# Attention and cosine router: router logits summed in the PSUM bank by token strips, and wide items' gates spread from bf16 parts

## The chip, the cores and the metric

The kernel runs on one core of a Trainium2 chip. The metric is device microseconds for one execution.

## The reference

An attention in which a query sees only the keys of its own cluster feeds a mixture of experts with a cosine router.

```
q_assign = argmax(q_n @ c_n.T); k_assign = argmax(k_n @ c_n.T)     # 16 clusters a head
scores = where(q_assign == k_assign, scale * q @ k.T, -1e9)         # 4 batches, 8 heads, 768 x 64
x = softmax(scores) @ v, put to (3072, 512)

logits = xn @ en.T / tau                    # xn, en: rows of length one; 8 experts
e = argmax(logits); gate = softmax(logits)[e]
out[token] = gate * (relu(x @ w1[e]) @ w2[e])                       # w1 512x1024, w2 1024x512
```

Everything is fp32.

## The kernel before, in words

The order of work on every engine is the order in which the program issues it (`tc.manual_schedule` over all five engines), so a wait on one engine holds up all that stands behind it there.

**Attention.** There are 16 pairs of heads, n = 4 b + nb for batch b. A pair has twelve units, done two at a time in six iterations (`it` 0 to 5). In an iteration PE makes the scores of the next two units (line 484), ScalarE takes their exponent (L495), PE attends two units (L506), and VectorE adds the exponents up (L525). Between them `between(n, it)` puts small pieces of other work: turning the keys and queries of later pairs, their cluster products (L396), and the router's work for the batch before, which is `route_pieces(b - 1)`. The sums over the keys are products with ones (L553), in `total`.

**The router's pieces.** When the four pairs of a batch are through, its rows lie turned in four tiles `xT[b, c]`, c = 0 to 3: 128 of the 512 features on the partitions, tokens along the row, in two halves of 384. `embT` holds the experts' vectors, 32 columns wide (8 used). `products(half)` makes four products of 384 columns, one per c, each into its own strip of 32 partitions of one bank (L628); ScalarE copies the bank to `pT` (L636). `logits(half)` turns this with three PE transposes into another bank (L641), and VectorE adds the four strips with one reduction into `lg` (L644). `choose` finds the best expert per token, marks it in `eq`, counts it in `cumx` on GpSimd, and subtracts the maximum from `lg`, which the gate needs later. For batches 0 to 2 these pieces stand at iterations (nb, it) = (0, 4), (0, 5), (1, 2), (1, 3) and (1, 4) of the batch that follows.

For the last batch there is no attention behind which to put them. `products(0)` stands at the end of the last iteration. Then the order is written out: the first early item's hidden layer, `total` of the last group, gate pieces of the first three batches (`gates[1]` to `gates[3]`, which go from VectorE to ScalarE and back), then

```
gates[3]()
weights1(E0[2])
logits(0)
read(0, NJ, P - SQ, P)
products(1)
hidden(E0[1], (0,))
logits(1)
choose()
```

**Banks.** `misc()` hands out two PSUM banks in turn to all small products: cluster products, totals, router products, transposes, tables, gates. Who writes a bank waits for the reader of its last use, two calls before.

**Experts.** After four early items, the list `later` holds 16 items: eight blocks of 128 tokens and eight sized (wide) items, of 272 tokens down to 160, as block, sized, sized, block, sized, ... For the sized ones the slots are laid out in pieces of 32 tokens with a quarter of the features, so that a piece's gate is needed on all four strips of 32 partitions. `pb.gates` brings the gates of all slots into `slot_gates` (128 x 22): 24 products (L988) give three bf16 parts of each gate, VectorE copies the bank to `g3` (L996) and adds the parts (L997, L998). `spread_gates` then makes `gates4` for the 14 columns of the sized items: 16 fp32 products with columns of the identity (L1187) and one VectorE copy (L1194). It is called once, inside `sized_result` of the first sized item (`later[1]`), after its last transposition from the bank (L1218) and ahead of the multiplication by `gates4` (L1234).

For each item the loop over `later` orders the second weights if it is sized (`order_w2`, L1159), turns the next item's rows, makes the hidden layer (L1174 sized, L1259 block), issues weight loads two items ahead on SP, and makes the result (L1209 sized, L1275 block).

Of the kernel before, what the change touches and what calls it, by code (L numbers as in the profile page):

```python
# [9 lines left out]
F32 = mybir.dt.float32  # L10
BF16 = mybir.dt.bfloat16
I32 = mybir.dt.int32
ALU = mybir.AluOpType
ACTF = mybir.ActivationFunctionType
AXX = mybir.AxisListType.X
# [3 lines left out]
P = 128  # L19

SQ = 32
# [13 lines left out]
def bc(ap, shape, axis):  # L35
    return ap.unsqueeze(axis).to_broadcast(shape)
# [3 lines left out]
def kernel(  # L40
# [12 lines left out]
    nc = tc.nc  # L53

    B, H, S, D = q.shape
    C = centroids.shape[1]
    E, DM = moe_expert_emb.shape
    F = moe_w1.shape[2]
    N = B * S
    NJ = S // P  # L60
    NHP = H // 2
    HS = S // 2
    NSLOT = N // P
    KD = DM // P
    KF = F // P
    NQ = P // SQ
# [11 lines left out]
    NS = -(-sum(WIDE) // NQ)  # L78
# [23 lines left out]
    ident = const.tile([P, P], F32, name="ident")  # L102
    identb = const.tile([P, P], BF16, name="identb")
    cnB = const.tile([P, NHP, 2 * C], F32, name="cnB")
    embT = const.tile([P, KD, 2 * C], F32, name="embT")
# [38 lines left out]
    smp = ctx.enter_context(tc.tile_pool(name="smp", bufs=2))  # L144
# [32 lines left out]
    def misc():  # L177
        return bank("misc", psM)
# [282 lines left out]
    xT = {}  # L461
# [156 lines left out]
    def route_pieces(b):  # L618

        own = slice(NJ * b, NJ * b + NJ)  # L620
        t = {"sq": sq_all[:, own], "lg": lg_all[:, own]}
        U = NJ // 2

        def products(half):

            bk = misc()
            for c in range(KD):
                nc.tensor.matmul(  # L628
                    bk[2 * C * c : 2 * C * c + 2 * C, 0:HS],
                    lhsT=embT[:, c],  # L630
                    rhs=xT[b, c][:, half],
                    start=True,
                    stop=True,
                )
            t["pT", half] = smp.tile([P, HS], F32, tag="pT", name="pT")
            nc.scalar.copy(t["pT", half], bk[:, 0:HS])  # L636

        def logits(half):
            bk = misc()
            for u in range(U):  # L640
                nc.tensor.transpose(  # L641
                    bk[:, P * u : P * u + P], t["pT", half][:, P * u : P * u + P], ident
                )
            nc.vector.tensor_reduce(  # L644
                t["lg"][:, U * half : U * half + U],
                bk[:, 0:HS].rearrange("p (u c e) -> p u e c", c=KD, e=2 * C)[:, :, 0:E],
                axis=AXX,
                op=ALU.add,
            )

        def read(j0, j1, c0=0, c1=P):
            if "xr" not in t:
                t["xr"] = xp.tile([P, NJ, NQ, P], F32, tag="xr", name="xr", bufs=1)
            rows = x_rows[S * b + P * j0 : S * b + P * j1].rearrange("(j p) x -> p j x", p=P)
            if c1 - c0 == P:
                nc.sync.dma_start(
                    out=t["xr"][:, j0:j1].rearrange("p j w x -> p j (w x)"), in_=rows
                )
                return
            for w in range(NQ):  # L660
                nc.sync.dma_start(
                    out=t["xr"][:, j0:j1, w, c0:c1], in_=rows[:, :, P * w + c0 : P * w + c1]
                )

        def norms(j):
            junk = smp.tile([P, DM], F32, tag="junk", name="junk", bufs=1)
            nc.scalar.activation(
                junk,
                t["xr"][:, j].rearrange("p w x -> p (w x)"),
                ACTF.Square,  # L670
                accum_out=t["sq"][:, j : j + 1],
            )

        shp = [P, NJ, E]

        def choose():
            s0 = NJ * b
            mx = smp.tile([P, NJ], F32, tag="mx", name="mx")
            sel = smp.tile(shp, BF16, tag="sele", name="sele")
            pm = smp.tile([P, NJ], BF16, tag="pme", name="pme")  # L680
            nc.vector.tensor_reduce(mx, t["lg"], axis=AXX, op=ALU.max)
            nc.vector.tensor_tensor(sel, t["lg"], bc(mx, shp, 2), ALU.is_equal)
            nc.vector.tensor_tensor(sel, sel, bc(prefe, shp, 1), ALU.mult)
            nc.vector.tensor_reduce(pm, sel, axis=AXX, op=ALU.max)
            nc.vector.tensor_tensor(eq[:, s0 : s0 + NJ], sel, bc(pm, shp, 2), ALU.is_equal)
            for s in range(s0, s0 + NJ):
                nc.gpsimd.tensor_tensor(cumx[:, s + 1], cumx[:, s], eq[:, s], ALU.add)
            nc.vector.tensor_tensor(t["lg"], t["lg"], bc(mx, shp, 2), ALU.subtract)

        return products, logits, read, norms, choose  # L690

# [60 lines left out]
    class Places:  # L752
# [230 lines left out]
        def gates(self, to):  # L983

            m = to.shape[1]
            bk = misc()[:, 0 : 3 * m]
            for s in range(self.slots):
                nc.tensor.matmul(  # L988
                    bk,
                    lhsT=self.oh[:, s],  # L990
                    rhs=self.rg[:, s].rearrange("p t k -> p (t k)"),
                    start=(s == 0),
                    stop=(s == self.slots - 1),
                )
            g3 = self.tile([P, 3, m], F32, f"g3{m}")
            nc.vector.tensor_copy(g3.rearrange("p t k -> p (t k)"), bk)  # L996
            nc.vector.tensor_tensor(to, g3[:, 0], g3[:, 1], ALU.add)  # L997
            nc.vector.tensor_tensor(to, to, g3[:, 2], ALU.add)  # L998
# [182 lines left out]
            nc.scalar.activation(d["hT"][:, f, 0:C], bk, ACTF.Relu)  # L1181

    def spread_gates():
        bk = misc()[:, 0 : NQ * NS]
        for w in range(NQ):
            for to in range(0, P, SQ):
                nc.tensor.matmul(  # L1187
                    bk[to : to + SQ, NS * w : NS * w + NS],
                    lhsT=ident[:, SQ * w : SQ * w + SQ],
                    rhs=slot_gates[:, 0:NS],  # L1190
                    start=True,
                    stop=True,
                )
        nc.vector.tensor_copy(  # L1194
            gates4.rearrange("p k w -> p w k"), bk.rearrange("p (w k) -> p w k", w=NQ)
        )

    def sized_result(it):

        d, C, n = mo[it], CAPS[it.j], WIDE[it.j]  # L1200
        ys = d["ys"] = szp.tile([P, max(WIDE), P], F32, tag="ys", name="ys")
        cut = KF - 2
        bks = {}

        def products(g, fs):
            if g not in bks:
                bks[g] = misc() if g >= 2 else bank("y_ps", psY)
            for f in fs:
                nc.tensor.matmul(  # L1209
                    bks[g][:, 0:C],  # L1210
                    lhsT=d["w2"][:, f, P * g : P * g + P],
                    rhs=d["hT"][:, f, 0:C],
                    start=(f == 0),
                    stop=(f == KF - 1),
                )

        def turn_back(g):
            nc.vector.transpose(  # L1218
                ys[:, 0:n, SQ * g : SQ * g + SQ],
                bks[g][:, 0 : SQ * n].rearrange("p (u t) -> p u t", t=SQ),  # L1220
            )

        products(0, range(cut))
        products(1, range(cut))
        for g in range(2):
            products(g, range(cut, KF))
            turn_back(g)
        for g in range(2, KD):
            products(g, range(KF))
            turn_back(g)  # L1230
        u0 = FIRST[it.j]
        if it is later[1]:
            spread_gates()
        nc.vector.tensor_tensor(  # L1234
            ys[:, 0:n], ys[:, 0:n], bc(flat(gates4)[:, u0 : u0 + n], [P, n, P], 2), ALU.mult
        )
# [85 lines left out]
    later = items[KA:]  # L1322
# [7 lines left out]
    def between(n, it):  # L1330
        b, nb = divmod(n, NHP)
# [22 lines left out]
        if b > 0:  # L1354
            if nb == 0 and it == 3:
                route[b - 1] = route_pieces(b - 1)
            products, logits, read, norms, choose = route.get(b - 1, (None,) * 5)


            m = NJ * nb + it  # L1360
            if m in (8, 11, 14):
                read((m - 8) // 3 * 2, (m - 8) // 3 * 2 + 2)
            if m in (15, 16, 18, 19, 21, 22):
                norms((15, 16, 18, 19, 21, 22).index(m))
            if (nb, it) == (0, 4):
                products(0)
            elif (nb, it) == (0, 5):
                products(1)
            elif (nb, it) == (1, 2):
                logits(0)  # L1370
            elif (nb, it) == (1, 3):
                logits(1)
            elif (nb, it) == (1, 4):
                choose()
        if n == NP - 1 and it == 4:
# [12 lines left out]
        if (n, it) in first:  # L1388
            w, j, i = first[n, it]
# [14 lines left out]
    with tc.manual_schedule(engines=by_hand):  # L1404
# [153 lines left out]
        for i, it in enumerate(later):  # L1558
# [30 lines left out]
                result(it)  # L1589
            if i == 0:  # L1590
                fetch(later[2])
            if i + 2 < LAST and it.kind != "sized":
                weights2(later[i + 2])
        if later[-1].kind == "sized":
# [44 lines left out]
```

## Time and profile before

| | |
|---|---|
| median of 8 runs | 721.09 us (720.54 to 724.16) |
| the profiled execution | 723.32 us, of which the span of its instructions is 721.5 us |
| granted TensorE clock over the span | 0.989 |
| busy: PE, VectorE, ScalarE, GpSimd | 97%, 53%, 37%, 37% |
| attention | up to about 341 us; the last PE product ends near 714 us |

How to read it: PE is TensorE's matmul, PEld its weight load, DVE VectorE, ACT ScalarE, POOL GpSimd, SP the engine that issues most transfers. A row of a group has the line, the engine, the operation, the tile written and those read, the shape and count, then the busy time, the mean length of one, and the engine's idle time ahead of them with what ended it. In the chain of what ended last each row has its start, the length of its slot, the engine and line, and the number of records; "issue" there is time in which the engine waited for nothing that the profile shows. In a row of busy time by stretch the last three figures are PE's granted clock, the busy share of the DMA engines and GB/s. An fp32 product shows as two weight loads and two matmul records, a bf16 product as one of each; a transposition shows as one of each.

### The profile page before, as it was taken

The page shows a single profiled execution, that of the slowest core. Times are in us where ns is not written, and L with a number is a line of the kernel's source. Part 1 is how long each engine was busy: PE and PEld are TensorE (multiplying, and loading weights), DVE is VectorE, ACT ScalarE, POOL GpSimd, SP SyncE. Part 2 cuts the span into 40 slices and gives each one's busy share as a digit, 9 for nine tenths or more (in the row PEclk, how much of TensorE's full clock was granted, in tenths as well). Part 3 has the DMA queues.
Part 4 walks back from the last instruction along what each step waited for, and adds up shares of the span by engine and source line. Part 5 has one row for each costly group of instructions (what it writes and reads, how often), then busy time and mean ns, then how long its engine had stood idle before and what let it go on. Part 6 is the DMA issues. An engine that isn't in the chain of part 4 may idle for free.

```text
span 721.5 us, 16021 instructions
## 1 busy us (share of the span) xinstructions
PE 701.7 (97%) x6462; PEld 458.3 (64%) x6462; DVE 381.7 (53%) x665; ACT 267.9 (37%) x454; POOL 263.7 (37%) x402
## 2 busy tenths in 40 slices
PE   7999999999999999999999999899999999999995
PEld 3444444444444444454966677797979797979693
DVE  4588887998979998998583111221030303031210
ACT  4556555577556655666315110101011111111111
POOL 2122221322224231444134446536355454535312
PEclk9899999999999999999999999999999999999998
DMA  9446556766547678669799977166848586869350
GB/s 145 72 68 108 104 100 96 143 146 112 96 88 154 128 144 164 141 179 332 176 306 351 332 261 273 36 252 237 298 168 302 213 315 218 313 234 332 131 217 28
DMA packets 244123, 135.53 MB, mean 188 GB/s; under 512 B 207808, under 2 KB 207810, under 8 KB 244044
## 3 DMA queue, kind: packets, MB, share of 16 engines
q1 hardware_dynamic: 237852, 121.28, 62.4%
q0 software_dynamic: 6016, 13.12, 5.2%
q8 instruction: 53, 0.87, 0.5%
q14 instruction: 26, 0.21, 0.1%
q10 hardware_dynamic: 176, 0.05, 0.0%
HBM read 115.92 MB, written 13.12 MB: 179 GB/s over the span
## 4 chain that ended last, share of the span: by engine, by line
PE 82%; issue 6%; DVE 5%; DMA 4%; POOL 1%; another core or an unknown queue 1%; ACT 1%; POOLq 0%; SPq 0%; DVEq 0%; ACTq 0%
PE s_ps L484 19%; PE o_ps L506 16%; PE h_ps L1259 10%; PE y_ps L1275 9%; PE h_ps L1174 9%; PE misc L1209 5%; PE y_ps L1209 5%; PE x_ps L1174 3%; DMA out_dram<-ys,spidx 3%; DVE acc L525 2%; PE misc L553 2%; PE misc L396 2%; PE misc L628 1%; DMA k<-in_k_dram 1%
## 5 line engine op out<-in xcount | busy, mean ns | idle before, releaser
L495 ACT ACTIVATE prob<-s_ps 128x768 f32<-128x768 f32 x192 | 153.4, 811 | 96.7 <-PE s_ps L484 76.8
L484 PE MATMUL s_ps<-qT,kT 64*64 64x384 f32 x1536 | 158.2, 486 | 0.0
L506 PE MATMUL o_ps<-prob,v 64*64 64x385 f32 x1536 | 144.5, 491 | 0.0
L525 DVE TENSOR_TENSOR acc<-acc,prob 128x768 f32<-128x768 f32 x128 | 125.2, 978 | 8.5 <-DVE acc L525 0.5
L506 PEld LDWEIGHTS o_ps<-prob,v 64*64 64x64 f32 x1536 | 54.9, 134 | 71.3 <-issue 60.0
L1259 PE MATMUL h_ps<-xTm,w1s 128*128 128x128 f32 x768 | 88.5, 275 | 1.7 <-issue 1.7
L1259 PEld LDWEIGHTS h_ps<-xTm,w1s 128*128 128x128 f32 x768 | 87.6, 192 | 4.1 <-issue 3.3
L539 POOL TENSOR_TENSOR o_sum<-o_sb 128x385 f32<-128x385 f32 x30 | 32.1, 1071 | 153.7 <-ACT o_sb L530 153.7
L1218 DVE STREAM_TRANSPOSE ys<-y_ps 128x256 f32<-128x256 f32 (+4 forms) x16 | 6.7, 416 | 154.0 <-PE y_ps L1209 153.0
L1275 PE MATMUL y_ps<-w2s,hT 128*128 128x512 f32 x192 | 85.0, 594 | 1.0 <-ACT hT L1266 1.0
L1050 POOL DMA_INDIRECT out_dram<-ys,spidx x56 | 56.9, 1016 | 76.6 <-DVE ys L1234 61.9
L484 PEld LDWEIGHTS s_ps<-qT,kT 64*64 64x64 f32 x1536 | 57.7, 134 | 38.1 <-issue 34.9
L1174 PE MATMUL h_ps<-xTs,w1s 128*128 128x272 f32 (+7 forms) x384 | 74.5, 351 | 1.0 <-ACTq L1539 1.0
L1266 ACT ACTIVATE hT<-h_ps 128x512 f32<-128x512 f32 x24 | 14.3, 596 | 160.8 <-PE h_ps L1259 118.4
L1174 PEld LDWEIGHTS h_ps<-xTs,w1s 128*128 128x128 f32 x384 | 67.7, 193 | 8.7 <-issue 2.9
L484 PE MATMUL s_ps<-hot 64*64 64x384 bf16 x768 | 66.1, 327 | 2.3 <-ACT prob L495 1.3
L574 POOL COPY inv<-inv 32x12 f32<-32x12 f32 x120 | 43.0, 358 | 55.0 <-DVE inv L571 50.6
L1039 POOL DMA_INDIRECT xs<-x_rows,gpidx x56 | 56.1, 1003 | 17.1 <-issue 16.8
L1275 PEld LDWEIGHTS y_ps<-w2s,hT 128*128 128x128 f32 x192 | 35.4, 190 | 41.8 <-issue 39.2
L484 PEld LDWEIGHTS <-hot 64*64 64x64 bf16 x768 | 24.1, 107 | 40.0 <-issue 38.9
L1209 PE MATMUL misc<-hTs,w2o 128*128 128x272 f32 (+7 forms) x256 | 48.0, 346 | 0.0
L1209 PE MATMUL y_ps<-hTs,w2o 128*128 128x272 f32 (+7 forms) x256 | 48.0, 346 | 0.0
(264 smaller groups left out, 690.2 us busy)
## 6 DMA issues: line engine op xcount, KB each, us to landing
w1s<-in_moe_w_dram SPq DMA_DIRECT2D x18, 2048.0 KB
w2s<-in_moe_w_dram SPq DMA_DIRECT2D x18, 2048.0 KB
v<-in_v_dram SPq DMA_DIRECT2D x128, 48.0 KB
q<-in_q_dram SPq DMA_DIRECT2D x60, 96.0 KB
k<-in_k_dram SPq DMA_DIRECT2D x60, 96.0 KB
x_rows<-xb SPq DMA_DIRECT2D x60, 96.0 KB
xr<-x_rows SPq DMA_DIRECT2D x9, 512.0 KB
w1s<-in_moe_w_dram SPq DMA_DIRECT2D x4, 1024.0 KB
```

Source lines behind the costliest of these rows:

```text
L484: nc.tensor.matmul(s_ps[D * half : D * half + D, h, 0:HS], lhsT=l[rows, half], rhs=r[rows], start=part == (1 if len(parts) < 2 else 0), st ...
L495: nc.scalar.activation(d["prob"][:, :, 0:HS], d["s_ps"][:, :, 0:HS], ACTF.Exp, scale=scale)
L506: nc.tensor.matmul(g["o_ps"][D * h : D * h + D, half, 0:HE], lhsT=ld[n]["v"][keys, j, h], rhs=d["prob"][keys, h, 0:HE], start=(j == 0), st ...
L525: nc.vector.tensor_tensor(g["acc"], g["acc"], d["prob"][:, :, 0:HS], ALU.add)
L539: add(t["o_sum"][:, hq], t["o_sb"][:, 0], t["o_sb"][:, 1], ALU.add)
L574: nc.gpsimd.tensor_copy(inv2[M * to : M * to + M, :, i % 2], inv[M * i : M * i + M])
L1039: nc.gpsimd.indirect_dma_start(out=to, out_offset=None, in_=of, in_offset=bass.IndirectOffsetOnAxis(ap=at, axis=0), bounds_check=n - 1, oo ...
L1050: inst = nc.gpsimd.indirect_dma_start(out=to, out_offset=bass.IndirectOffsetOnAxis(ap=at, axis=0), in_=of, in_offset=None, bounds_check=n - 1,
L1174: nc.tensor.matmul(bk, lhsT=w1s[it.slot][:, c, P * f : P * f + P], rhs=d["xT"][:, c, 0:C], start=(c == 0), stop=(c == KD - 1),)
L1209: nc.tensor.matmul(bks[g][:, 0:C], lhsT=d["w2"][:, f, P * g : P * g + P], rhs=d["hT"][:, f, 0:C], start=(f == 0), stop=(f == KF - 1),)
L1259: nc.tensor.matmul(bk[:, m : m + P], lhsT=w1s[it.slot][:, c, f0 + m : f0 + m + P], rhs=d["xT"][:, P * c : P * c + P], start=(c == 0), stop ...
L1275: nc.tensor.matmul(bk, lhsT=d["hT"][:, P * c : P * c + P], rhs=w2s[it.slot][:, c], start=(c == 0), stop=(c == KF - 1),)
```

## The change

**Router.** `products(*halves)` now takes one or two halves. A strip of 32 partitions no longer holds one c, but the tokens of one quarter of each 128 (32 w to 32 w + 31); the four c are added up in the bank. So there are 16 products, of 192 columns for both halves together or of 96 for one. `logits(*halves)` is a single VectorE transposition of 32x32 blocks from that bank to a new tile `lt`; the copy on ScalarE, the PE transposes and the reduction are gone, and `choose` reads `lt`. For batches 0 to 2 both halves go together, products at (0, 4) and logits at (0, 5). For the last batch the calls stay as they were, one half at a time.

**Gates of the wide items.** `gates` copies the bank also as bf16 to `g3b`; `spread_gates` spreads the three bf16 parts (42 columns) with the bf16 identity instead of the fp32 gates (14 columns), and VectorE copies the bank and adds the parts. It is called after the first later item's result instead of inside the first sized item's.

```
-        def products(half):
-
-            bk = misc()
+        def products(*halves):
+
+            J = U * len(halves)
+            bk = t["bk", halves[0]] = misc()
             for c in range(KD):
-                nc.tensor.matmul(
-                    bk[2 * C * c : 2 * C * c + 2 * C, 0:HS],
-                    lhsT=embT[:, c],
-                    rhs=xT[b, c][:, half],
-                    start=True,
-                    stop=True,
-                )
-            t["pT", half] = smp.tile([P, HS], F32, tag="pT", name="pT")
-            nc.scalar.copy(t["pT", half], bk[:, 0:HS])
-
-        def logits(half):
-            bk = misc()
-            for u in range(U):
-                nc.tensor.transpose(
-                    bk[:, P * u : P * u + P], t["pT", half][:, P * u : P * u + P], ident
-                )
-            nc.vector.tensor_reduce(
-                t["lg"][:, U * half : U * half + U],
-                bk[:, 0:HS].rearrange("p (u c e) -> p u e c", c=KD, e=2 * C)[:, :, 0:E],
-                axis=AXX,
-                op=ALU.add,
+                x = xT[b, c][:, halves[0] : halves[0] + len(halves)]
+                x = x.rearrange("p k (u w t) -> p w k u t", w=NQ, t=SQ)
+                for w in range(NQ):
+                    nc.tensor.matmul(
+                        bk[SQ * w : SQ * w + SQ, 0 : SQ * J],
+                        lhsT=embT[:, c],
+                        rhs=x[:, w],
+                        start=(c == 0),
+                        stop=(c == KD - 1),
+                    )
+
+        def logits(*halves):
+            J = U * len(halves)
+            if "lt" not in t:
+                t["lt"] = smp.tile([P, NJ, SQ], F32, tag="lt", name="lt", bufs=1)
+            nc.vector.transpose(
+                t["lt"][:, U * halves[0] : U * halves[0] + J].rearrange("p j e -> p (j e)"),
+                t.pop(("bk", halves[0]))[:, 0 : SQ * J],
             )
...
+            lt = t["lt"][:, :, 0:E]
+            nc.vector.tensor_reduce(mx, lt, axis=AXX, op=ALU.max)
+            nc.vector.tensor_tensor(sel, lt, bc(mx, shp, 2), ALU.is_equal)
...
+            nc.vector.tensor_tensor(t["lg"], lt, bc(mx, shp, 2), ALU.subtract)
...
             g3 = self.tile([P, 3, m], F32, f"g3{m}")
+            if self.part == 1 and m == self.blocks:
+                self.g3b = self.tile([P, 3, m], BF16, "g3")
+                nc.vector.tensor_copy(self.g3b.rearrange("p t k -> p (t k)"), bk)
...
     def spread_gates():
-        bk = misc()[:, 0 : NQ * NS]
+
+        bk = misc()[:, 0 : NQ * 3 * NS].rearrange("p (w t k) -> p w t k", w=NQ, t=3)
         for w in range(NQ):
             for to in range(0, P, SQ):
                 nc.tensor.matmul(
-                    bk[to : to + SQ, NS * w : NS * w + NS],
-                    lhsT=ident[:, SQ * w : SQ * w + SQ],
-                    rhs=slot_gates[:, 0:NS],
+                    bk[to : to + SQ, w],
+                    lhsT=identb[:, SQ * w : SQ * w + SQ],
+                    rhs=pb.g3b[:, :, 0:NS],
                     start=True,
                     stop=True,
                 )
-        nc.vector.tensor_copy(
-            gates4.rearrange("p k w -> p w k"), bk.rearrange("p (w k) -> p w k", w=NQ)
-        )
+        parts = mop.tile([P, 3, NS, NQ], F32, tag="parts4", name="parts4", bufs=1)
+        nc.vector.tensor_copy(parts.rearrange("p t k w -> p w t k"), bk)
+        nc.vector.tensor_tensor(gates4, parts[:, 0], parts[:, 1], ALU.add)
+        nc.vector.tensor_tensor(gates4, gates4, parts[:, 2], ALU.add)
...
-        if it is later[1]:
-            spread_gates()
...
             if (nb, it) == (0, 4):
-                products(0)
+                products(0, 1)
             elif (nb, it) == (0, 5):
-                products(1)
-            elif (nb, it) == (1, 2):
-                logits(0)
-            elif (nb, it) == (1, 3):
-                logits(1)
+                logits(0, 1)
...
             if i == 0:
                 fetch(later[2])
+                spread_gates()
```

More of the change, by code (lines that the diff above doesn't have):

```diff
@@ L680, in choose @@
             pm = smp.tile([P, NJ], BF16, tag="pme", name="pme")
-            nc.vector.tensor_reduce(mx, t["lg"], axis=AXX, op=ALU.max)
-            nc.vector.tensor_tensor(sel, t["lg"], bc(mx, shp, 2), ALU.is_equal)
+            lt = t["lt"][:, :, 0:E]
+            nc.vector.tensor_reduce(mx, lt, axis=AXX, op=ALU.max)
+            nc.vector.tensor_tensor(sel, lt, bc(mx, shp, 2), ALU.is_equal)
             nc.vector.tensor_tensor(sel, sel, bc(prefe, shp, 1), ALU.mult)
@@ L687, in choose @@
                 nc.gpsimd.tensor_tensor(cumx[:, s + 1], cumx[:, s], eq[:, s], ALU.add)
-            nc.vector.tensor_tensor(t["lg"], t["lg"], bc(mx, shp, 2), ALU.subtract)
+            nc.vector.tensor_tensor(t["lg"], lt, bc(mx, shp, 2), ALU.subtract)
         return products, logits, read, norms, choose
```

## The prediction

> **What bounds the kernel now.** I read the page's busy times first, to see which engine could set the end:
>
> ```profile
> PE 701.7 (97%) x6462; PEld 458.3 (64%) x6462; DVE 381.7 (53%) x665; ACT 267.9 (37%) x454; POOL 263.7 (37%) x402
> ```
>
> PE is busy from end to end, so what leaves PE's queue is worth its full length, unless PE then waits for somebody. A share is not yet a place, so next come the groups kept apart by form, for the lines the change touches:
>
> ```profile
> L628 PE MATMUL misc<-xT,embT 128*32 128x384 f32 x64 | 6.8, 498 | 0.0
> L641 PE MATMUL misc<-ident,pT 128*128 128x128 f32 x24 | 4.3, 286 | 0.0
> L644 DVE TENSOR_REDUCE lg_all<-misc 128x24 f32<-128x96 f32 x8 | 1.9, 238 | 3.8 <-PE misc L641 3.8
> L1187 PE MATMUL misc<-slot_gates,ident 128*32 128x14 f32 x32 | 1.1, 186 | 3.0 <-issue 3.0
> ```
>
> An fp32 matmul is two records (32 products give 64). Means overlap, so what a group costs PE's queue is read from the chain that ended last, in order of time. Around batch 2's router work:
>
> ```profile
> 276.16 0.78 PE misc L628 x8
> 276.94 1.45 PE o_ps L506 x16
> ...
> 286.10 0.81 PE misc L553 x16
> ...
> 291.56 0.48 PE misc L641 x3
> 292.03 1.45 PE o_ps L506 x16
> ...
> 298.65 1.29 PE o_ps L506 x16
> ```
>
> The reader should see the slot of each insertion, and that the attend after it takes 1.45 instead of 1.29: an insertion costs 0.16 more. Then the gate spread, by the same view:
>
> ```profile
> 449.74 0.32 PE misc L1187 x25
> 450.06 0.56 issue
> 450.62 0.17 PE misc L1187
> 450.79 0.54 issue
> 451.33 0.22 PE misc L1187 x3
> 451.56 1.89 issue
> 453.44 0.29 PE misc L1187 x3
> 453.73 6.96 PE h_ps L1174 x24
> ```
>
> Sixteen tiny products hold PE from 449.74 to 453.73, 3.99 us. The busy time by stretch says what follows:
>
> ```profile
> 449.00:454.00 5.00, 2.01 (x37) 1.38 (x36) 0.52 (x2) 0.00 (x0) 2.01 (x3) 0.95 0.24 67
> 454.00:458.00 4.00, 4.00 (x13) 3.24 (x13) 3.97 (x10) 0.38 (x1) 1.92 (x2) 0.64 0.05 16
> ```
>
> The clock column falls to 0.64 after the stop, and the next 24 hidden products take 6.96 where the 24 from 462.42 take 5.18: 1.78 more. Last, VectorE's timeline at the end of attention, needed for a wait that the change makes:
>
> ```profile
> 352.63 0.21 DVE L717 STREAM_TRANSPOSE gate_t<-gate_p 128x32 f32<-128x32 f32 x1
> 352.77 0.21 DVE L644 TENSOR_REDUCE lg_all<-misc 128x24 f32<-128x96 f32 x1
> ```
>
> **Batches 0 to 2 of the router.** Before, per batch: two product slots of 0.78 + 0.16 and two turns of 0.48 + 0.16, together 3.16 us of PE. After: 16 products of 192 columns in one slot. The nearest row is L553, also 192 columns on 32-column strips: 16 records in 0.81, where its records in the trace start four at a time, 0.162 apart. The change has 32 records, four groups more: 0.81 + 4 x 0.162 = 1.46, plus 0.16 = 1.62. Bounds: 1.46 if the insertion costs nothing extra; and, if sums within a bank kept strips from overlapping, 32 x 0.162 = 5.2. I take 1.62, since L553's strips overlap as wanted and L396 reads runs of 32 elements no slower than whole rows. Saved: 1.54 per batch, 4.62 in three.
>
> ScalarE loses two copies of 0.48 per batch. VectorE loses two reductions of 0.24 and gains a transpose of 128x192: 0.38 by the L1218 form of that size, also from a bank. All that lies beside PE; if that cover went, VectorE would still come out 0.1 ahead. `choose` reads the same 48 numbers with a longer stride; bounds -0.1 and +0.3 for its three reads, taken as 0. What is late next is VectorE's additions: in its timeline it idles only 0.2 and 0.47 between 204 and 251, and the chain runs over it from 224.8 to 264.8. Of the 1.28 that PE loses in that pair of heads, VectorE can follow with 0.67 + 0.48 = 1.15. With a little more for ScalarE's waits I take **4.4** of the 4.62.
>
> **The last batch.** Here the halves stay apart: `products(0)`, later `logits(0)`, `products(1)`, a hidden half, `logits(1)`. A half is now 32 records of 96 columns. [...] The L1187 row above has 25 records in 0.32, 13 ns each, on four strips. The trace decides: four records per 0.081 (half of L553's 0.162), 0.65 plus L553's start of 0.16, 0.81 against 0.78 now. [...]
>
> The new cost is a wait. `misc` has two banks in turn. Before: `products(0)` X, `total` Y, `logits(0)` X, `products(1)` Y. After, `logits(0)` takes no bank, so `products(1)` gets X, which is free only when VectorE has transposed the first half, and that stands behind `gates[3]` in its queue: L717 ends at 352.84, the transpose of 128x96 takes 0.28 (0.35 at 160 columns, 0.38 at 192, carried down), with a hand-over 353.2. PE arrives at 350.98 and waits 2.2 us; queued behind it are the hidden half of the second early item and everything after. `products(1)` then ends at 354.06 instead of 352.09: +1.97. The second turn (0.33 in the chain at 355.86) goes: net **+1.65**. `choose` comes earlier, but nobody on PE waits for it. SP's and POOL's queues keep their order and only shift with PE.
>
> Could the pause halve the clock? A stop of 1.74 at 407.67 did not (clock 1.00 in that stretch), the one at 450 did; 2.2 lies between. [...]
>
> **The gate spread.** After: 16 bf16 products of 42 columns, behind the result of the first later item. The nearest row is L1024, 16 of 44 columns: 0.21 in the chain, with the hidden block after it 0.20 longer, so 0.41. Bounds: -0.2 and the 3.99 of today. If the stop belongs to this burst of 64 fp32 loads and products, 3.99 + 1.78 - 0.41 = **5.36** is gained; L1024's 32 instructions show no stop. VectorE gains a copy of 0.23 (as L996) ahead of a gate that ScalarE needs only at 420.49, then a copy of 0.49 (as L1032) and two additions of about 0.2, and it loses the 0.22 copy L1194. The eight weight-ordering copies (L1159, 2.8 us at 415.37) now stand behind them and behind the result: about 421.6 to 424.4. Their reader is PE at 435.07, so 10 us of hidden products cover it; without cover it would be 4 to 6 us.
>
> **Sum.** -4.4 + 1.65 - 5.36 = -8.1 us. It is made against the profiled execution (723.32, span 721.5); the median of 8 runs is 2.2 lower, so a stop such as the 1.74 at 407.67 may be missing there, but not all of the 7.5 that the two stops and the slow clock cost. I take the sum off the median: 721.09 - 8.1 = 713.0, say 713.2.
>
> **Rivals.** *The stop is not the burst's.* The records say only "issue", and the stop at 407.67 has no burst; both come while transfers fill the DMA engines (share 0.95 in 403 to 410, 1.02 in 446 to 449). Then it returns elsewhere or was in the profile alone: -4.4 + 1.65 = -2.75, so 718.4. *VectorE bounds attention.* It is 90% busy there; if batches 0 to 2 give only 1.0, the sum is -4.7: 716.4. Against: the chain runs over PE before 204 and after 264.8. *Slower: the new product bursts stop PE.* Each is 64 loads and products in one go, as L1187's was. At 3.6 + 1.8 us each, and with the old stop staying, one gives 718.4 + 5.4 = 723.8, three 734.6; it decides from one stop without the gain at the spread, or two with it. Against: wide products drain slowly, and L553's 32 instructions run without a gap. *The change does not do what it says*: the spread's fp32 products vanish in any case, so only the sizes are in doubt.
>
> **How the numbers follow.** All as worked out 0.50 (713.2, own range 711.3 to 715); stop stays or is not in ordinary runs 0.30 (717 to 720); VectorE bound 0.08; bursts that stop PE 0.12 (above 722). Range 711.3 to 720.0 leaves out the last case and a little at the low end. A measurement of this kernel can tell about 0.2%, 1.4 us, from no change. Faster 0.82, same 0.07, slower 0.11.
>
> **What would show it.** Right: one L628 slot per batch near 1.46 and none of L641; attends of 1.29 there; a PE gap of about 2 us before the second half's products, released by VectorE; the spread under 0.5 us at about 420, and clock 1.0 near 450. Wrong: pauses marked "issue" in or after the L628 bursts, VectorE in the chain through all of attention, or a stop still near 450.

## The result, and the profile after

The changed kernel takes 715.3 us (median of 11 runs, 712.97 to 720.36) where the kernel before takes 721.6 (median of 32): a ratio of 0.9914, 95% interval 0.9897 to 0.9931, or 6.2 us less (5.0 to 7.4). The forecast was 713.2, so the direction and the range held, the sum promised 2 us more than came, and the time lies just above 715, where the case "all as worked out" ended. The profiled execution took 718.94 us with a span of 717.2, against 723.32 and 721.5.

The busy times come first, as before:

```profile
PE 694.8 (97%) x6518; PEld 456.8 (64%) x6518; DVE 382.0 (53%) x665; ACT 264.3 (37%) x446; POOL 262.8 (37%) x402
```

PE has lost 6.9 us of work and still fills 97% of the span, so PE still sets the end. The changed lines, in the groups kept apart by form (after the bar: busy time, mean ns of one; then the idle time before them):

```profile
L632 PE MATMUL misc<-xT,embT 128*32 128x192 f32 x96 | 4.5, 329 | 0.0
L632 PE MATMUL misc<-xT,embT 128*32 128x96 f32 x64 | 1.7, 249 | 2.1 <-DVE lt L644 2.1
L644 DVE STREAM_TRANSPOSE lt<-misc 128x192 f32<-128x192 f32 x3 | 1.0, 339 | 0.0
L644 DVE STREAM_TRANSPOSE lt<-misc 128x96 f32<-128x96 f32 x2 | 0.5, 262 | 1.0 <-PE misc L632 1.0
L1198 DVE COPY parts<-misc 128x168 f32<-128x168 f32 x1 | 0.5, 468 | 6.4 <-PE misc L1190 6.4
```

The products of batches 0 to 2 waited for nobody; those of the last batch waited 2.1 us for VectorE's transpose. The chain that ended last shows the slot of batch 0 (start, length, what), and the places where the two turns used to stand:

```profile
109.95 1.44 PE misc L632 x32
111.39 1.45 PE o_ps L506 x16
112.85 1.61 PE s_ps L484 x24
114.46 1.29 PE o_ps L506 x16
...
125.06 1.29 PE o_ps L506 x16
...
127.97 1.29 PE o_ps L506 x16
```

One slot of 1.44, one attend of 1.45 behind it, and the attends where turns were inserted are back at 1.29. Now the last batch, by the chain, by PE's waits (total, times, longest) and by the busy time of stretches (PE, PEld, DVE, ACT, POOL, then the granted clock, DMA share, GB/s):

```profile
345.26 0.21 DVE gate_t L716
345.47 0.18 DVE lt L644
...
345.69 0.87 PE misc L632 x32
346.56 5.39 PE h_ps L1261 x32
```
```profile
PE misc L632 <- DVE lt L644: 2.1, 1, 2.1
```
```profile
344.00:346.50 2.50, 0.81 (x33) 0.66 (x33) 1.15 (x6) 0.81 (x2) 0.00 (x0) 1.00 0.54 80
346.50:350.00 3.50, 3.50 (x21) 3.50 (x18) 1.40 (x7) 0.00 (x0) 1.19 (x6) 0.54 0.30 52
```

The chain leaves PE here and runs over VectorE: the gate's last step (L716), the transpose (L644), and only then the products. Right behind the pause the clock column falls to 0.54, and the hidden half of 32 products takes 5.39. This fall is what the prediction left out. Last, the spread and the place at 450:

```profile
409.06 6.95 PE y_ps L1277 x16
416.01 0.21 PE misc L1190 x16
416.22 5.70 PE h_ps L1176 x24
...
438.41 7.33 PE misc L1213 x32
445.75 5.18 PE h_ps L1176 x24
```
```profile
450.00:454.00 4.00, 4.00 (x20) 3.51 (x19) 4.00 (x9) 1.06 (x4) 2.06 (x2) 1.00 0.05 16
```

The spread takes 0.21, the hidden block behind it 5.70, and where PE had stood for 3.99 us the first sized item's products now run straight into the next hidden block, at full clock.

The two traces can be cut at PE instructions that both have: the first cluster product (L396) of each pair of heads, and the first y product of each sized item (L1209, now L1213). The stretches between the cuts, in us:

| stretch | before | after | difference |
|---|---|---|---|
| up to the second pair of heads | 25.04 | 22.32 | -2.7 |
| batches 0 to 2 | 279.36 | 274.44 | -4.9 |
| last batch, the early items, up to the first sized result | 130.51 | 134.16 | +3.65 |
| from that result to the next | 34.26 | 28.48 | -5.8 |
| the next four sized results | 152.90 | 158.08 | +5.2 |
| the rest | 99.47 | 99.68 | +0.2 |

The second, third and fourth differences are the change. The first is not: in the profile of before the clock was halved from 16.6 to 23.4 us, in that of after it was not, and of the seven variants below three have no such stretch and four have one (what decides it is told with the clock below). Nor is most of the fifth, which holds a stop of 2.04 us that lasts 0.65 in two of the variants and that the others do not have:

```profile
601.19 0.60 ACT L1268 ACTIVATE hT<-h_ps 128x512 f32<-128x512 f32 x1 [7.77 <-remote]
601.84 2.86 PE L1277 MATMUL y_ps<-w2s,hT 128*128 128x512 f32 x4 [2.04 <-ACT hT L1268]
```

PE waits here for ScalarE, which itself starts 4.8 us after the end (596.36) of the hidden product that it reads. The clock is halved until 606.2, and the stretch from one sized item's first y product to the next takes 39.68 where it takes 35.67 in before, 35.66 or 35.67 in five variants, and 36.6 in the two with the short stop. No run ties this stop to the change. The difference of the two profiled executions, 4.4 us, is therefore a sum of chances as well as of the change; the stages and the medians have to be read apart.

### The profile page after: what moved, and what is told of

Its sections match the earlier page's. It is cut to its first block, busy times and chain, and to the rows that moved or that the text cites. A ratio compares the mean times of both kernels' runs of the same rounds, so it can differ in the third digit from the quotient of the medians.

```text
span 717.2 us, 16122 instructions
## 1 busy us (share of the span) xinstructions
PE 694.8 (97%) x6518; PEld 456.8 (64%) x6518; DVE 382.0 (53%) x665; ACT 264.3 (37%) x446; POOL 262.8 (37%) x402
## 4 chain that ended last, share of the span: by engine, by line
PE 80%; DVE 5%; issue 5%; DMA 4%; another core or an unknown queue 2%; ACT 1%; POOL 1%; SPq 1%; POOLq 0%; DVEq 0%; ACTq 0%
PE s_ps L484 19%; PE o_ps L506 15%; PE y_ps L1277 9%; PE h_ps L1176 9%; PE h_ps L1261 9%; PE misc L1213 5%; PE y_ps L1213 5%; DMA out_dram<-ys,spidx 3%; PE x_ps L1176 3%; PE misc L553 2%; PE misc L396 2%; DVE acc L525 2%; PE misc L632 1%; DMA k<-in_k_dram 1%
## 5 line engine op out<-in xcount | busy, mean ns | idle before, releaser
L484 PE MATMUL s_ps<-qT,kT 64*64 64x384 f32 x1536 | 156.0, 482 | 0.0
L506 PE MATMUL o_ps<-prob,v 64*64 64x385 f32 x1536 | 142.0, 486 | 0.0
L1261 PE MATMUL h_ps<-xTm,w1s 128*128 128x128 f32 x768 | 90.4, 279 | 1.3 <-issue 1.3
L1261 PEld LDWEIGHTS h_ps<-xTm,w1s 128*128 128x128 f32 x768 | 89.1, 195 | 3.0 <-issue 2.6
L1277 PE MATMUL y_ps<-w2s,hT 128*128 128x512 f32 x192 | 87.3, 605 | 3.8 <-ACT hT L1268 3.1
L484 PEld LDWEIGHTS s_ps<-qT,kT 64*64 64x64 f32 x1536 | 56.0, 133 | 38.0 <-issue 34.9
L1176 PE MATMUL h_ps<-xTs,w1s 128*128 128x272 f32 (+7 forms) x384 | 72.9, 346 | 1.1 <-ACTq L1537 1.1
L1213 PE MATMUL misc<-hTs,w2o 128*128 128x272 f32 (+7 forms) x256 | 48.2, 346 | 0.1
L1213 PE MATMUL y_ps<-hTs,w2o 128*128 128x272 f32 (+7 forms) x256 | 48.0, 346 | 0.0
```

The costliest lines, as they stand in the source:

```text
L484: nc.tensor.matmul(s_ps[D * half : D * half + D, h, 0:HS], lhsT=l[rows, half], rhs=r[rows], start=part == (1 if len(parts) < 2 else 0), st ...
L506: nc.tensor.matmul(g["o_ps"][D * h : D * h + D, half, 0:HE], lhsT=ld[n]["v"][keys, j, h], rhs=d["prob"][keys, h, 0:HE], start=(j == 0), st ...
L1176: nc.tensor.matmul(bk, lhsT=w1s[it.slot][:, c, P * f : P * f + P], rhs=d["xT"][:, c, 0:C], start=(c == 0), stop=(c == KD - 1),)
L1213: nc.tensor.matmul(bks[g][:, 0:C], lhsT=d["w2"][:, f, P * g : P * g + P], rhs=d["hT"][:, f, 0:C], start=(f == 0), stop=(f == KF - 1),)
L1261: nc.tensor.matmul(bk[:, m : m + P], lhsT=w1s[it.slot][:, c, f0 + m : f0 + m + P], rhs=d["xT"][:, P * c : P * c + P], start=(c == 0), stop ...
L1277: nc.tensor.matmul(bk, lhsT=d["hT"][:, P * c : P * c + P], rhs=w2s[it.slot][:, c], start=(c == 0), stop=(c == KF - 1),)
```

## The experiments

All are small edits of the kernel before or after. The router alone, the moved fp32 spread, the bf16 spread at the old place and the other bank shared a chip and runs of before (median 720.82); the doubled products, the gathers and the earlier transpose shared another (721.11).

### The router alone

The kernel after, with the spread of before at its place of before:

```
-            if self.part == 1 and m == self.blocks:      # bf16 parts
-                self.g3b = ...
         if it is later[1]:
+            spread_gates()                               # 16 fp32 products
```

> The router part of the change alone: the gate spread stays as it was before (fp32, inside the first sized item's result). Both theories: attention gains about 4.9 us by the slots, the last batch gives back 3.1 (the wait for the bank and a slow clock after it), so 1.6 to 1.8 less than before, about 719.9. Theory 'the stop belongs to the spread as it was': its stop of about 4 us and the slow clock stay near 445, and the kernel is 4.5 to 5.4 us slower than the whole change. Rival 'stops come at random and the profile of before caught one there': no stop at the spread, and a time within 1 us of the whole change (715 to 716).

Measured: 723.81 us, ratio 1.0043 (1.0029 to 1.0057). Batches 0 to 2 lose their time as in after, step for step. The last batch, up to the first sized result, takes 134.60, 4.1 more than before, with a pause of 2.1 and a slow clock as in after. And the stop is back, in the chain:

```profile
445.71 0.35 PE misc L1186 x26
446.06 1.20 issue
447.26 0.23 PE misc L1186 x3
447.49 1.20 issue
```

So nothing in the router part took the stop away. By its stages (-4.9, +4.1 and -0.2) the kernel would be 1 us faster than before, and it is 3 us slower. Its profile shows one more PE stop of 0.92 us:

```profile
681.38 0.90 PE L1173 MATMUL h_ps<-xTs,w1s 128*128 128x160 f32 x2 [0.92 <-ACT hTs L1180]
```

It stands behind the code of the overflow branch, which is skipped, and just behind 16 KB fetches of instructions (to 677.0 and to 680.2); the clock is 0.52 in the 3.5 us that follow, and the stretch between the two sized items there takes 37.18 instead of 34.22. That would be 3.0 of the missing 4 us if the ordinary runs have it too, which nothing shows; they have a mean granted clock of 0.989, against 0.993 for those of before. The rest was not traced to a place.

### The fp32 spread, moved and nothing else

The kernel before, with `spread_gates()` where the change puts it:

```
-        if it is later[1]:
-            spread_gates()
...
                 fetch(later[2])
+                spread_gates()
```

> Before, with the fp32 gate spread only moved to after the first later item's result, its 64 loads and products as they were. Theory 'form' (the burst of 64 small fp32 instructions stops PE): a stop of about 4 us and a slow clock come at about 420 instead of 450, time as before (721 to 722). Rival 'place' (what stands around it near 450 makes the stop): no stop, 5.4 us faster than before, about 716.

Measured: 716.64 us, 0.9933 (0.9912 to 0.9954). The chain:

```profile
419.22 0.37 PE misc L1187 x32
419.59 5.70 PE h_ps L1174 x24
```

The same 32 fp32 records that held PE for 3.99 us take 0.37 here. There is no stop at 450 either: from the first sized result to the next it takes 28.48, exactly as in after. The fp32 form alone does not make the stop; the place does, or the form in that place. Moving this one call, with nothing else of the change, takes 4.8 us (3.3 to 6.3) off.

### The bf16 spread at the old place

The kernel after, with `spread_gates()` put back to its place of before.

> The whole change, with the bf16 gate spread called at the old place, inside the first sized item's result. Theory 'form': no stop, within 0.5 us of the whole change, about 715.3. Rival 'place': the stop of about 4 us and the slow clock are back near 445, about 720.5.

Measured: 715.73 us, 0.9931 (0.9909 to 0.9954), 0.4 above after, which is less than can be told apart. The chain:

```profile
445.15 0.21 PE misc L1190 x16
445.36 2.79 PE h_ps L1176 x12
448.15 0.72 issue
448.87 2.85 PE h_ps L1176 x12
```

Half the records pass, and PE goes on for 3 us, but it still stands for 0.72 twelve hidden records later, and from the first sized result to the next it takes 29.86, 1.4 more than in after. So either half of the edit is enough to be rid of most of the stop, and what stops PE depends on how much is issued behind something. The next run tests that.

### The bf16 spread at the old place, each product twice

The variant above with the same results written twice, so that the form stays bf16 and the number of records is that of the fp32 spread:

```
+                for _ in range(2):
                     nc.tensor.matmul(bk[to : to + SQ, w], ...)
```

> The bf16 gate spread at the old place (as in e4_bf16_old_place), with every one of its 16 products issued twice: 64 small records instead of 32. What stands behind it: in all profiles so far the completion signal of the product ahead of the spread reaches VectorE 3.7 us late, and PE goes on until some 60 records stand behind that product. Theory 'count': 64 records use that up at once, so the stop grows from 0.7 to about 3.4 us, with the slow clock behind it: 4 to 5 us slower than e4_bf16_old_place, about 720. Rival 'fp32': it was the fp32 form, so doubled bf16 products cost only their own 0.2 us: about 716.

Measured: 721.38 us, 1.0003 (0.9982 to 1.0024), 5.65 above the variant with single products. The chain:

```profile
445.02 0.36 PE misc L1191 x25
445.38 1.22 issue
446.61 0.24 PE misc L1191 x3
446.85 1.18 issue
```

The picture is that of fp32 in before: about 25 records go through, then it stands, 1.22, 1.18 and 0.52 us. At this place the number of records decides, not their type. (About 1.2 us of the 5.65 are another PE stop, of 0.93 us at 679, of the kind seen at 680 above.)

What PE stands behind is seen on VectorE, in its timeline. Its turn of the last product ahead of the spread starts, in this order, in after and in the bf16 variant with single products at the old place,

```profile
449.48 0.48 DVE L1222 STREAM_TRANSPOSE ys<-misc 128x288 f32<-128x288 f32 x1 [6.69 <-PE h_ps L1176]
```
```profile
448.91 0.48 DVE L1222 STREAM_TRANSPOSE ys<-misc 128x288 f32<-128x288 f32 x1 [6.69 <-remote]
```

and in before:

```profile
453.48 0.48 DVE L1218 STREAM_TRANSPOSE ys<-misc 128x288 f32<-128x288 f32 x1 [6.66 <-remote]
```

Those products end at 445.75, 445.15 and 449.74, so VectorE, idle for over 6 us, starts 3.7 us late in all three. In the trace of before the semaphore by which PE signals the product's end moves at 453.45, so it is the signal that is late, not VectorE. The late signal is there with and without the stop. What differs is what PE has to issue meanwhile. Counted in the traces between that product and the signal: 61 loads and products in before, 62 in the router alone, 37 in after and in the moved fp32 spread, whose hidden products are wide and slow (24 in 5.18 us in after). PE runs on while the signal is out; it first stands 50 to 52 records behind the product in the three kernels with 64 small records, 56 in the bf16 variant with 32, and the signal comes at 58 to 62. A few records can be missing from a trace. What sets these counts no run here shows.

Two limits. A wait for instructions is no rival here: in before no fetch of instructions lies between 435.6 and 459.3. But the count is not all there is: the stop between 400 and 410, which every profile has (0.7 to 1.9 us; 1.74 at 407.67 in before), also stands behind a signal that is about 2.4 us late, yet with 4 to 13 records behind the product. That stop stays unexplained.

### The gathers put elsewhere

The kernel before, with the gathers of one later item sent behind the first sized item's scatters, so that they are not in flight at 450:

```
-            if i > 0 and i + 2 < len(later) and ...:
+            if i > 0 and i != 2 and i + 2 < len(later) and ...:
                 fetch(later[i + 2])
...
                 send(later[i - 1])
+            if i == 2:
+                fetch(later[i + 2])
```

> Before, with the gathers of the fifth later item's rows (eight indirect transfers that GpSimd issues from 441.5 to 451.6) put behind the first sized item's scatters, so that none is on its way while the gate spread runs. Theory 'gathers' (the completion signal is late because the gathers' own signals come slowly then): VectorE's last turn of that item starts on time, at about 449.8 instead of 453.5, no stop, about 5 us faster than before, 716. Rival 'the burst alone', or weights: the stop and the late signal stay, time as before (721).

Measured: 726.76 us, 1.0082 (1.006 to 1.0104); nearly 11 us above what was expected. The chain and VectorE's timeline at the spread:

```profile
448.29 0.37 PE misc L1187 x32
448.67 5.38 PE h_ps L1174 x24
```
```profile
448.33 0.48 DVE L1218 STREAM_TRANSPOSE ys<-misc 128x288 f32<-128x288 f32 x1 [3.18 <-PE misc L1209]
```

Here the old spread at its old place passes in 0.37, and VectorE follows 0.04 us after the product. The DMA engines are busy for 0.42 of 445 to 450, where they were full in before up to 449. So the late signal goes when the gathers go. It comes back where they went: VectorE's next turn starts 11 us after the end of the last y product (469.58), and in the chain PE now stands among single products,

```profile
480.75 0.78 DVE L1218 STREAM_TRANSPOSE ys<-y_ps 128x256 f32<-128x256 f32 x2 [26.77 <-remote]
```
```profile
469.80 0.90 issue
470.70 0.38 PE misc L1209
471.07 2.41 issue
```

and in 470 to 480 it is busy for 2.70 of 10 us, with the DMA engines full:

```profile
470.00:480.00 10.00, 2.70 (x6) 1.60 (x7) 0.00 (x0) 0.00 (x0) 6.18 (x7) 0.72 1.03 388
```

The stretch between the two sized results takes 52.31 instead of 40.78. There the gathers run beside the weight loads.

Full DMA engines are not what a late signal needs. In before they are busy for only 0.19 of the wait itself, 449.74 to 453.45, while the last of the gathers go out; in after, where ScalarE starts 4.8 us late at 601.19, they are busy for 0.10 of 598 to 602 while GpSimd sends the scatters. Counted in the nine traces between 20 and 700 us, a completion signal of PE came more than 0.7 us late 141 times. In 140 of these an indirect transfer (a gather or scatter that GpSimd sends) was being issued between the product's end and its signal, or less than 1.5 us before; some 700 signals in such places were on time within 0.2 us, and some 2,890 elsewhere. In 84 of the 141 the DMA engines were busy for less than 0.35. So the late signal goes with indirect transfers, in this edit and in the count; how they hold it up is not settled.

### The other bank for the second half

The kernel after, with one bank skipped, so that `products(1)` need not wait for the transpose:

```
         read(0, NJ, P - SQ, P)
+        misc()
         products(1)
```

> The whole change, with one turn of the two banks skipped ahead of the last batch's second products, so that they get the bank that the totals used and need not wait for VectorE's transpose. Theory 'the wait and the half clock after it cost 3.6 us': about 711.7, PE's gap of 2.1 gone and the hidden half behind it 3.8 instead of 5.4. Rival 'the slow clock after the wait is a matter of the window's phase, not of the wait': 713.3 at best. Rival 'PE waits for VectorE later anyway': 715.3.

Measured: 711.39 us, 0.9876 (0.9851 to 0.9901); 3.9 below after. The chain:

```profile
341.41 3.57 PE h_ps L1261 x32
344.98 0.80 PE misc L632 x32
345.78 3.77 PE h_ps L1261 x32
```

No pause; the hidden half takes 3.77 instead of 5.39, 1.62 less. The stretch up to the first sized result is 130.69, 3.5 less than in after. One line that issues nothing gives back both the wait and the slow clock, and this kernel beats both others.

### The first half's transpose ahead of gates[3]

The kernel after, with the order on VectorE turned instead of the bank:

```
+        logits(0)
         gates[3]()
         weights1(E0[2])
-        logits(0)
```

> The whole change, with VectorE's transpose of the last batch's first half put ahead of the third gate piece in its queue. Both theories: PE's wait falls from 2.08 to about 0.75 us. Theory 'a pause of 0.75 does not slow the clock, one of 2.1 that lies within one window does': 1.3 us plus the 1.6 of the slow clock in the runs that had it, so 712.3 to 714. Rival 'any pause there slows the clock': 714.0, with a clock of one half for 3.4 us behind it in the profile.

Measured: 713.17 us (four runs), 0.9889 (0.9848 to 0.9931). The chain:

```profile
344.96 0.21 DVE lt L644
...
345.21 0.87 PE misc L632 x32
346.08 3.77 PE h_ps L1261 x32
```

PE still waits for the transpose, from 344.55 to 345.21, but 0.66 instead of 2.08, and the hidden half takes 3.77: this pause does not cost any clock. So the 1.62 does not come with the new products, which stand here too; it went when 1.4 us of the pause went.

## Why the prediction was right, and where it was too low

**Batches 0 to 2: 4.4 taken, 4.9 measured.** The slot was sized at 1.46 from L553 and takes 1.44; the surcharge of 0.16 on the next attend is there once per batch. The pairs of heads with router work lose 1.58, 1.79 and 1.57 (of the 1.79, 0.23 lies in the pairs just behind), to 0.02 us the same in the variants. The step that was off is the cut from 4.62 to 4.4 for VectorE's additions: VectorE followed with all of it, and the rival "VectorE bounds attention" has nothing in its favour. The estimates for VectorE's transposes, 0.38 and 0.28, measured 0.34 and 0.26.

**Last batch: the wait was right, the clock was not.** The forecast had a wait of 2.2 for the bank behind `gates[3]`, and the traces have 2.08, with VectorE's transpose as its releaser. A half of 32 records of 96 columns measured 0.80 without a pause (0.87 behind one) against 0.81 by the row: for records on four column strips the row was right. The failed step is the clock: the sum adds nothing for it, and no run shows that a pause of 2.2 leaves it alone. Here 2.08 us of idleness are followed by 3.4 us at half clock, +1.62 by the hidden half of after (5.39 against 3.77), and the slow clock is there too in the three variants that kept this wait; without the pause, or with 0.66, there is none. Other stops of nearly 2 us, such as the 1.74 at 407.67 in before, were followed by no slow clock.

The traces say more. The slow stretches lie on a raster of 3.413 us, whose steps are the windows that two of the expectations speak of: the clock falls at 16.59 and 453.50 in before, 128 steps apart, and at 346.81 and 602.81 in after, 75 steps apart, and each stretch lasts whole steps (6.83 and 3.41 us in before, 3.41 twice in after). In all four kernels the 2.08 lay inside one step, while the stop at 407.67 crossed an edge and left 1.46 in its step. PE's idle time can be added up step by step in the nine traces, up to 700 us. All fourteen steps at full clock with 1.97 us or more of it (2.08 and 2.96 in before, 2.08 and 2.04 in after) were followed by a step at half clock. Of those with less, one was (1.77, in the router alone), and others, with 1.86 and 1.75, were not. So what counts, as far as these traces show, is the sum inside one step, and the limit lies near 1.8 to 2.0 us. This also decides the first row of the table of stretches: the pauses between 13 and 17 us add up to 2.08 in one step in before, and an edge splits them into 1.39 and 1.43 in after. No run here moved a pause across an edge on purpose.

The stage gives +3.65: 0.41 for the spread, 1.62 for the clock, and the rest, 1.62, is the +1.65 of the forecast.

**The spread: 5.36 forecast, 5.37 measured.** From the first sized result to the next the time falls by 5.78, the 3.99 of the stop and the 1.78 of the slow clock, and 0.41 is paid earlier (0.21, and 5.70 instead of 5.50 behind it). "If the stop belongs to this burst of 64 fp32 loads and products" was right as to the burst and too narrow as to fp32: it needs the burst's number of records and a late signal ahead of it. The size was right because the whole stop left with the burst, not because fp32 had made it. Its copy of 0.49 measured 0.47, and nobody on PE waited for what VectorE does there.

**The sum against the medians.** By stages the change gives -4.9 + 3.65 - 5.8 = -7.0 us, the forecast's -8.1 with 1.6 for the clock added and the half microsecond of the batches taken off. The medians give -6.2 (5.0 to 7.4). Taking a sum from one profile off a median assumed that ordinary runs have that profile's stops and clock, and they have not all: 39 runs of before made beside the experiments have mean granted clocks from 0.989 to 0.998, and over them 0.001 of clock goes with 0.57 us (correlation -0.90). One stretch of 3.4 us at half clock is 0.0024 of the mean, 1.4 us by that slope. Runs of both kernels can differ by some of these, as a pause falls inside a step or across an edge. Nor do the parts add up in the medians: the router alone is 3.1 us slower than before, the fp32 spread moved alone 4.8 faster, and both parts together 6.2 faster. How much of the gain is the router's in ordinary runs therefore stays open; by the stages of the profiles it is 1.7, which is 4.9 less the 3.24 of wait and slow clock.

**Rivals.** That a burst of products stops PE was true of a burst of this size behind a late signal, and of none of the new router bursts, which are 64 loads and products each too; no late signal was seen ahead of them. That the stop is not the burst's was half true: the late signal lies in front of the burst, and yet the stop leaves when the burst leaves.

## What to carry to other kernels

When a step stops using a buffer from a ring of two, every later user of the ring lands on another bank: follow the ring, ask what stands in the releaser's queue ahead of the release, and skip a bank where that costs less than the wait. A stop marked "issue" on an engine that waits for nothing can lie behind a completion signal that is late (by 3.7 us here): look at the consumer's start against the producer's end, count the records between them, and put few and long instructions into such a place. Price a pause of about 2 us on PE with and without the 1.6 us of slow clock that followed 2.08 here, add up short pauses that lie close together (those between 13 and 17 us made 2.08 in one step of 3.4 us in before), and compare stages with stages, since two profiles also differ in stops that belong to neither kernel.

## What the runs showed of the hardware that was not expected

- A completion signal of PE reached VectorE 3.7 us and ScalarE 4.8 us after the product's end, while GpSimd sent gathers or scatters, with the DMA engines busy for only 0.19 and 0.10; at the spread PE went on for 50 to 56 records behind the product before it first stood.
- The clock fell by steps of a raster of 3.413 us: after each of fourteen steps with 1.97 us or more of PE idleness, after one with 1.77, and not after others with 1.86 or 1.75. A pause of 2.08 us inside one step cost 1.62 us of slow clock; one of 1.74 that crossed an edge cost none.
- Behind a skipped branch PE stood for 0.92 and 0.93 us in two of the variants, with the clock at 0.52 afterwards in one; that it waits for instructions there is likely from the fetches just ahead of it, and was not tested.
